# Turning the normed input by transposing DMAs instead of TensorE, in a fused convolution and gated-product kernel

## The chip, the cores and the metric

The kernel runs on one core of one Trainium2 chip. The core has TensorE (matrix products; the profile shows its matmuls as PE and its weight loads as PEld), VectorE (DVE), ScalarE (ACT), GpSimd (POOL) and SyncE (SP, which here only issues DMAs), and 16 DMA engines that all queues share. The metric is device time in microseconds of the whole launch. A time is given as the median of several executions; a profile is of one execution.

## The reference

The output is the sum of the input, a long convolution branch and a gated branch, both fed with the layer-normed input. Cut to what matters:

```python
x  = A_q                                   # 1 x 2048 x 640, bfloat16
xn = (x - mean(x)) / sqrt(var(x) + 1e-5)   # over the last axis

# A: short shift convolution of k (4 taps), times v, long convolution over 2048 tokens, times xn
kv = shift(k, shift_k) * v
y  = irfft(rfft(kv, 4096) * rfft(ssm_k, 4096))[:2048] + kv * ssm_D
A  = xn * y

# B: gated product
h  = sigmoid(xn @ w_gate) * (xn @ w_up)    # 640 x 1728 each
B  = h @ w_down                            # 1728 x 640

out = x + A + B
```

## The kernel before

**Layout.** Token 16 p + b lies on partition p in block b, so x and xn are tiles of 128 partitions x 16 blocks x 640 columns. Four blocks make a group (512 tokens), and there are four groups, t or g from 0 to 3. The 640 columns are five pieces of 128, counted by c, both as the contraction of the gated branch and as the five channel chunks of the convolution.

**Gated branch, by group.** `ln_norms`, `ln_var`, `ln_pow` and `ln_xn` norm a group's four blocks (VectorE, with one power on GpSimd). A product over columns needs the tokens of a block turned, columns on partitions. `xn_mm(g, i)` turns block i of group g by five TensorE transposes into a PSUM tile `pt`, and `xn_ev` copies it to `xnT[:, i]` on ScalarE. There is only one `xnT`, of four blocks; a group's turns write it after the last product of the group ahead has read it. Then 13 pairs `gate_mm`, `up_mm` (each five matmuls over 512 tokens) and one joint `both_mm` for the last 64 columns of both; `gate_ev` takes the sigmoid on ScalarE, `up_ev` multiplies on VectorE into `hT`. After that comes the group's down stage: eight `down_mm` products of 14 matmuls, in two pieces of seven each, evicted by `down_ev` (VectorE, added to x). The first group is handled ahead of the loop, with its turns between quarter products.

**Convolution branch, by chunk c.** It is a transform in two stages of matmuls. `kv_op` (16 VectorE steps) makes the shifted k times v, and `h_turn` rearranges the filter. `st1_mm` (8 steps of 8 matmuls) is the first stage; `st1_ev` evicts each to a tile `t`, `wr1` writes it to DRAM and `rd2` reads it back regrouped. `st2_mm` and `st2_ev` are the second stage, `prod` multiplies the spectra (VectorE), `inv1_mm`, `inv1_ev`, `wr2`, `rdb` and `inv2_mm` go back, and `inv2_q` and `inv2_x` multiply by xn and add to x. All evictions `st1_ev`, `st2_ev` and `inv1_ev` are ScalarE copies of 128x1024 f32.

**Order.** Each engine runs its instructions in program order. `step(k, fn, ...)` appends steps to chains by letter, and the string `ORDER` merges the chains by hand: each letter takes the next step of its chain. The letters F, J, I and Y take a step of B, C, A and E, but with its copy on VectorE; before's string has none of them. The SP queue issues nearly all DMAs, also in program order: a DMA that waits holds all that stand behind it.

**Letters that matter here.** g: gate, up, both and down products; s and u: their evictions; l and P: norms; e and E: `xn_mm` and `xn_ev` of groups 1 to 3; a and A, b and B, c and C: the three transform stages and their evictions; w, r, W, R: their DMAs; m, n, h, K, V, T: loads; k: `kv_op`; p: `prod`; d and q: `inv2`; o: stores.

**Buffers.** PSUM has two pools: `psC`, two buffers, for the transform stages (and the turns of the first group), and `psG`, four buffers, for products, down products, `inv2` and the turns of groups 1 to 3. The tiles `t1` and `t2` of the transform have two buffers each; `hn`, `sraw` and `dr` have one.

Of the kernel before, what the change touches and what calls it, by code (L numbers as in the profile page):

```python
# [10 lines left out]
BF16 = mybir.dt.bfloat16  # L11
# [8 lines left out]
P = 128  # L20
NB = S // P
NC = DM // P
# [35 lines left out]
def kernel(  # L58
# [14 lines left out]
    nc = tc.nc  # L73
# [17 lines left out]
    psC = ctx.enter_context(tc.tile_pool(name="psC", bufs=2, space=bass.MemoryType.PSUM))  # L91
    psG = ctx.enter_context(tc.tile_pool(name="psG", bufs=4, space=bass.MemoryType.PSUM))

    ident = res.tile([P, P], BF16, name="ident")
# [11 lines left out]
    xn = res.tile([P, NB, DM], BF16, name="xn")  # L106
    xnT = res.tile([P, 4, NC, P], BF16, name="xnT")
# [13 lines left out]
    sync = nc.sync  # L121
# [105 lines left out]

    xts = {}

    def xn_mm(g, i):  # L230
        pool, tag = (psG, "g") if g else (psC, "c")
        xts[i] = pt = pool.tile([P, NC, P], BF16, name="pt", tag=tag)
        for c in range(NC):
            nc.tensor.transpose(pt[:, c, :], xn[:, 4 * g + i, c * P:(c + 1) * P], ident[:])  # L234

    def xn_ev(g, i, copy=act_copy):
        copy(out=xnT[:, i, :, :], in_=xts[i][:, :, :])


    sig = {}  # L240
# [246 lines left out]
            nc.tensor.matmul(idle[:, :], lhsT=hT[:, 0, 0:P], rhs=hT[:, 0, :], start=True, stop=True)  # L487

    def turn(i):
        xn_mm(0, i)  # L490
        xn_ev(0, i)


    busy(15)
    for i in range(4):
# [5 lines left out]
        ln_pow(0, i, i + 1)  # L501
    ln_xn(0, 3)
    turn(0)
    busy(2)
    for i in range(4):
        for fc in range(2):
            for u in range(2):
                quarter(u, fc, i)
            if (i, fc) in ((0, 0), (1, 0), (1, 1)):
                turn(1 + i + fc)  # L510
# [2 lines left out]
        up_ev(0, fc)  # L513


    chains = {k: [] for k in "ABCDEHKPRTVWZabcdeghklmnopqrstuw"}

    def step(k, fn, *args):
        chains[k].append((fn, args))
# [88 lines left out]
    for g in range(1, 4):  # L608
        for i in range(4):
            step("l", ln_norms, g, i)  # L610
        step("l", ln_var, g, 0, 4)
        step("P", ln_pow, g, 0, 4)
        for i in range(4):
            step("l", ln_xn, g, i)
        for i in range(4):
            step("e", xn_mm, g, i)
            step("E", xn_ev, g, i)

    for b in range(0, 12, 2):
        step("o", store, b, b + 2, 0, 4 * P)  # L620
# [5 lines left out]
    step("o", store, NB - 1, NB, 4 * P, DM)  # L626

    ORDER = """
    mmmmmmmmmmZgmgsmgumgsmgugsgugsmgugskgkugkskgumkgsmkgumkgsmTguHgsHDgumgskkgukgskmgukgskgumkgkmgmutmkm
    auTaAHgAHDagAwlhauaAlglaglguwlgkPkgAulgAllleKeuKwEekaEekaEgkEVVHAgAHDgwughkgkugkskguKrrkaskaAgkAkguw  # L630
    gkskgutkgTskgkKuKaksaAKkgAkaugAwkaksaAkgkwakAgVuAVHasgwHDAauhgAkgkskwbugBrkgBkktbgpBrTkgBpsapsaAuguA
    apKgKswAkaugAkaKkwsakgVHAVgAuDHgswkcugCkgkskCgnuWakaAkgAkgukwbguBrlgBlgulbgBrlgBuglkPpgnulgllleenuEe
    kbEeprgEEgptkBgupBgkaauAgpAkapgswAkaugAkawksaAgkAkguwlcsglCgClbusgrlBWgBkugslpPkaauAgllAlglspwbgBruR
    kgBkscpguCpgCksWbkgBrugBkksbpgBrudBpdgsRqpcqgCqugCqpsWbgBrukgBspbgBrupdBadqsaApRgqAqapgwAqauseeEueaE
    egEEgAgAwaudAdqgwqRqcugCqgCguWbgBrgBugpbpdBrdqgBuqgqpcqgCupgCguWbgBrgBugpspRbgBrugBspcguCpgsCguWbsdr
    BdqgRBqqguqbpsgrBpgBugpspcgCugCsWbguBrdBgqspbqgBupgBspgucpsdCgRqRCqguWbsgBgBugpspgudsdqcqgCqoqdCudqg
    WqqgsqgugoguRRguggugguogodudqogqqogqdoudqogqqogqguogooouo
    """
    left = {k: iter(v) for k, v in chains.items()}
    for k in "".join(ORDER.split()):  # L640
# [33 lines left out]
```

## Time and profile before

| | us |
|---|---|
| median of 3 runs | 240.34 (239.64 to 241.22) |
| the profiled execution, whole | 240.16 |
| its span in the trace | 238.4 |
| TensorE, matmuls busy | 232.6 |
| VectorE busy | 190.5 |
| ScalarE busy | 140.9 |

The span runs from the first to the last instruction that the profiler records; the time of the whole execution has 1.8 us around it. The first product starts at about 8.3 us, when the first loads are in, and TensorE's last at 235.1. The granted TensorE clock is 1.00 throughout.

Matmuls of one kind that follow one another overlap: a transpose of 128x128 is recorded with 219 ns, and five of them in a row take 0.28 us in the chain. A product of five matmuls over 512 tokens takes 1.08 us. So a busy share of 98% does not mean that TensorE works at its peak, but an idle time in front of an instruction does mean that it waited.

The DMA issues are listed with their size and the median time from issue to landing; the queue's share of 16 engines' span counts the time of its packets.

### The profile page before, as it was taken

What the parts mean: (1) busy time and instruction counts of PE and PEld (TensorE: products, weight loads), DVE (VectorE), ACT (ScalarE), POOL (GpSimd) and SP (SyncE); (2) the same over time, 40 slices, a digit from 0 to 9 for tenths busy, and PEclk for the clock granted to TensorE, in tenths of its full rate; (3) what the DMA queues carried; (4) which work ended last, traced back from release to release, by engine and by line L of the source; (5) the groups of instructions that cost most, each with busy time, mean ns of one, the idle gap of its engine ahead of it and who ended that gap; (6) DMA issues with size and microseconds to landing.
All of it is one profiled execution on the core that took longest, in us unless ns stands there. A gap on an engine that the chain in (4) does not pass through costs nothing.

```text
span 238.4 us, 5555 instructions
## 1 busy us (share of the span) xinstructions
PE 232.6 (98%) x2265; PEld 134.8 (57%) x2265; DVE 190.5 (80%) x350; ACT 140.9 (59%) x178; POOL 11.2 (5%) x24
## 2 busy tenths in 40 slices
PE   8899999999999999999999999999999999999994
PEld 2664445877555555667754434577664434456772
DVE  4633989999999999999999999865585695968372
ACT  2343322728557898764888787997558858764000
POOL 5210000020000000002000000000000000000000
PEclk9999999999999999999999999999999999999999
DMA  7999999998998999998444889875849795285494
GB/s 213 291 315 236 254 326 294 197 257 236 251 312 252 259 292 292 297 252 313 154 179 143 235 237 265 216 231 202 230 119 223 186 282 126 83 241 145 123 303 137
DMA packets 89119, 54.82 MB, mean 230 GB/s; under 512 B 47814, under 2 KB 83206, under 8 KB 88838
## 3 DMA queue, kind: packets, MB, share of 16 engines
q1 hardware_dynamic: 88150, 53.66, 81.3%
q10 hardware_dynamic: 944, 0.82, 1.1%
q8 instruction: 17, 0.28, 0.5%
q14 instruction: 8, 0.07, 0.1%
HBM read 36.12 MB, written 18.35 MB: 228 GB/s over the span
## 4 chain that ended last, share of the span: by engine, by line
PE 91%; DMA 5%; ACT 2%; issue 0%; ACTq 0%; DVE 0%
PE pd L301 26%; PE pg L257 22%; PE pu L257 22%; PE psb L461 4%; PE ps L360 3%; PE ps L362 3%; PE ps L393 3%; DMA w<-in_B_w_up_dram 3%; PE psa L422 2%; PE pg L278 2%; PE pt L234 2%; DMA d<-t 2%; ACT t L223 1%; PE pu L248 1%; PE pg L248 1%
## 5 line engine op out<-in xcount | busy, mean ns | idle before, releaser
L257 PEld LDWEIGHTS <-w 128*128 128x128 bf16 x500 | 46.4, 98 | 54.4 <-issue 5.3
L301 PE MATMUL pd<-wd,hT 128*128 128x320 bf16 (+2 forms) x448 | 64.3, 299 | 0.0
L257 PE MATMUL pg<-xnT,w 128*128 128x512 bf16 x250 | 62.2, 379 | 0.0
L257 PE MATMUL pu<-xnT,w 128*128 128x512 bf16 x250 | 62.2, 379 | 0.0
L301 PEld LDWEIGHTS <-hT 128*128 128x128 bf16 x448 | 42.3, 98 | 18.5 <-issue 1.7
L266 ACT ACTIVATE sig<-pg 128x512 bf16<-128x512 f32 x52 | 31.3, 605 | 29.8 <-PE pg L257 28.0
L272 DVE TENSOR_TENSOR hT<-sig,pu 128x512 bf16<-128x512 bf16 x52 | 35.2, 680 | 15.5 <-PE pu L257 9.6
L223 ACT CAST t<-ps 128x1024 bf16<-128x1024 f32 x40 | 39.2, 1023 | 12.1 <-DMA d<-t 7.9
L223 ACT CAST xz<-ps 128x1024 bf16<-128x1024 f32 x40 | 38.5, 1017 | 10.6 <-PE ps L393 10.5
L306 DVE TENSOR_TENSOR x<-pd,x 128x320 bf16<-128x320 f32 (+2 forms) x32 | 15.3, 479 | 15.5 <-PE pd L301 15.3
L408 DVE TENSOR_TENSOR xz<-xz 128x2048 bf16<-128x2048 bf16 x20 | 24.3, 1217 | 0.2
L360 PE MATMUL ps<-kvh,S1t 128*128 128x128 bf16 x160 | 21.2, 217 | 0.5 <-ACT t L223 0.5
L362 PE MATMUL ps<-kvh,S1t 128*128 128x128 bf16 x160 | 21.2, 220 | 0.0
L340 DVE TENSOR_TENSOR acc<-acc,tmp 128x1024 bf16<-128x1024 bf16 x30 | 20.7, 689 | 0.6
L338 DVE TENSOR_TENSOR tmp<-kx,sc 128x1024 bf16<-128x1024 bf16 x30 | 20.5, 685 | 0.4
L223 ACT CAST ao<-psa 128x1024 bf16<-128x1024 f32 x16 | 15.6, 1014 | 6.0 <-PE psa L422 3.9
L362 PEld LDWEIGHTS <-S1t 128*128 128x128 bf16 x160 | 15.4, 96 | 2.9 <-issue 0.8
L466 DVE TENSOR_TENSOR yx<-psb,xn 128x512 bf16<-128x512 f32 x20 | 13.8, 690 | 3.9 <-PE psb L461 2.9
L360 PEld LDWEIGHTS <-S1t 128*128 128x128 bf16 x160 | 15.5, 97 | 2.3
L223 ACT COPY xnT<-pt 128x640 bf16<-128x640 bf16 x16 | 10.2, 708 | 10.9 <-PE pt L234 10.6
L198 DVE BATCH_NORM_STATS2 st<-x 128x6 f32<-128x320 bf16 x32 | 13.7, 470 | 2.6 <-DMA x<-in_A_q_dram 2.6
L406 DVE STREAM_SHUFFLE xz<-xz 128x512 f32<-128x512 f32 x20 | 14.5, 725 | 0.0
(44 smaller groups left out, 147.5 us busy)
## 6 DMA issues: line engine op xcount, KB each, us to landing
d<-t SPq DMA_DIRECT2D x20, 512.0 KB, 3.9
t<-d SPq DMA_DIRECT2D x20, 512.0 KB, 5.2
bi<-d SPq DMA_DIRECT2D x8, 512.0 KB, 5.2
d<-ao SPq DMA_DIRECT2D x6, 512.0 KB, 4.1
kx<-in_A_k_dram SPq DMA_DIRECT2D x10, 256.0 KB, 5.1
hn<-in_A_ssm_k_dram SPq DMA_DIRECT2D x20, 128.0 KB, 5.9
kvh<-in_A_v_dram SPq DMA_DIRECT2D x10, 256.0 KB, 5.3
x<-in_A_q_dram SPq DMA_DIRECT2D x3, 640.0 KB
```

The source lines that it names most:

```text
L223: nc.scalar.copy(out=out, in_=in_)
L257: nc.tensor.matmul(pg[:, :], lhsT=w[:, c, u * UP + fc * P:u * UP + (fc + 1) * P], rhs=xnT[:, :, c, :], start=(c == 0), stop=(c == NC - 1))
L266: nc.scalar.activation(sig[fc][:, :], pgs[0, fc][:, :], ACT.Sigmoid)
L272: nc.vector.tensor_tensor(hT[:, fc, :], sig[fc][:, :], pgs[1, fc][:, :], ALU.mult)
L301: nc.tensor.matmul(pd[:, :], lhsT=hT[:, fc, bb * P:(bb + 1) * P], rhs=wd[:, fc, es], start=(fc == 0), stop=(fc == NFC - 1))
L306: nc.vector.tensor_tensor(x[:, 4 * t + bb, es], pds[bb, half][:, :], x[:, 4 * t + bb, es], ALU.add)
L338: nc.vector.tensor_tensor(d["tmp"][:, :, :], kx[:, lo + 3 - m:hi + 3 - m, :], sb(m), ALU.mult)
L340: nc.vector.tensor_tensor(d["acc"][:, :, :], d["acc"][:, :, :], d["tmp"][:, :, :], ALU.add)
L360: nc.tensor.matmul(ps[:, i, 0:P], lhsT=S1[:, b, h, :], rhs=cin[c]["kvh"][:, 0, b, :], start=True, stop=True)
L362: nc.tensor.matmul(ps[:, i, P:2 * P], lhsT=S1[:, b, h, :], rhs=hp[:, b // 2, b % 2, :], start=True, stop=True)
L406: nc.vector.stream_shuffle(z[:, 2, :, :].bitcast(F32), z[:, 1, :, :].bitcast(F32), swap)
L408: nc.vector.tensor_tensor(z[:, 1:3, :, :], z[:, 0:1, :, :].to_broadcast((P, 2, 8, P)), z[:, 1:3, :, :], ALU.mult)
```

## The change

The turns of groups 1 to 3 are made by a transposing DMA on the SP queue, one for each block of 128 tokens x 640 columns, from `xn` straight to `xnT`. The 12 `xn_mm` and 12 `xn_ev` steps go, with their PSUM tiles; the turns of group 0 remain as they were. Letter E is gone, and e now stands for the DMA.

The order string is another one, in all its length. Each chain keeps its own order; what differs is how the chains are merged. Fourteen evictions now run on VectorE: seven `inv1_ev` (J), five `st2_ev` (F) and two `st1_ev` (I).

```diff
-    def xn_mm(g, i):
-        pool, tag = (psG, "g") if g else (psC, "c")
-        xts[i] = pt = pool.tile([P, NC, P], BF16, name="pt", tag=tag)
+    def xn_mm(i):
+        xts[i] = pt = psC.tile([P, NC, P], BF16, name="pt", tag="c")
         for c in range(NC):
-            nc.tensor.transpose(pt[:, c, :], xn[:, 4 * g + i, c * P:(c + 1) * P], ident[:])
+            nc.tensor.transpose(pt[:, c, :], xn[:, i, c * P:(c + 1) * P], ident[:])
-    def xn_ev(g, i, copy=act_copy):
-        copy(out=xnT[:, i, :, :], in_=xts[i][:, :, :])
+    def xn_ev(i):
+        nc.scalar.copy(out=xnT[:, i, :, :], in_=xts[i][:, :, :])
+    def xn_turn(g, i):
+        sync.dma_start_transpose(xnT[:, i, :, :], xn[:, 4 * g + i, :])
...
         for i in range(4):
-            step("e", xn_mm, g, i)
-            step("E", xn_ev, g, i)
+            step("e", xn_turn, g, i)
```

Where the turns stand, in the order of the SP queue around them (st1, st2 and gate steps are TensorE's, at their place in the string):

| group | before | after |
|---|---|---|
| 1 | `xn_mm` 0 to 3 after the down pieces of block 2, between `st1_mm(0, 5)` and `st1_mm(0, 7)` | SP: wr1(0,1), load h of chunk 2, **turns 0 to 3**, wr1(0,2); turn 3 stands between `st1_mm(1, 1)` and the first gate product |
| 2 | after the down pieces of block 2, around `st2_mm(4)` | SP: load k of chunk 4, wr1(2,2), **turn 0**, rd2(3), wr1(2,3), load h of chunk 4, rd2(4), **turns 1 to 3**, wr1(3,0), rd2(5) |
| 3 | ahead of the down products, around `st1_mm(4, 6)` | SP: rd2(11), **turn 0**, wr1(4,1), rdb(1,0), rd2(12), **turns 1 to 3**, rdb(1,1) |

Other steps that change their place among the chains: in group 1's down stage `st1_mm(0, 0)` to `st1_mm(0, 3)` stand between the first down pieces, not behind four of them; `st1_mm(1, 0)` and `st1_mm(1, 1)` go ahead of the first gate product of group 1; `ln_norms` of group 1 go ahead of the first four `down_ev`, and its four `ln_xn` stand among `kv_op` and `down_ev` steps, not in a row; the norms of group 2 go ahead from the down stage of group 1 into its products. The first `rd2` moves from gate product 1 to gate product 5 of group 1; `st2_mm(0)` stays behind up product 7. `prod` 9 and 10 and three `inv2` evictions move from group 2's products to its down stage. The loads of h, k, v and taps of chunks 2 to 4 mostly come later in the SP queue, among the `wr1` and `rd2` steps, and those of x of groups 2 and 3 earlier. The first 19 loads keep their order.

More of the change, by code (lines that the diff above doesn't have):

```diff
@@ L489, in turn @@
     def turn(i):
-        xn_mm(0, i)
-        xn_ev(0, i)
+        xn_mm(i)
+        xn_ev(i)
     busy(15)
@@ L513 @@
         up_ev(0, fc)
-    chains = {k: [] for k in "ABCDEHKPRTVWZabcdeghklmnopqrstuw"}
+    chains = {k: [] for k in "ABCDHKPRTVWZabcdeghklmnopqrstuw"}
     def step(k, fn, *args):
@@ L628 @@
     ORDER = """
[L629 to L637, printed above, removed]
+    mgmmmmgmgmgsummZmgmgsmmgugmssgkmmukgskgugkusgsugkkgkHggmmuskuggkHmssukgmDgggukskgukkksaTmmgauAgmkaAH
+    HlglAalAlglmwgautAkagugmggPmwlkgAhglkelauleggkakukkugekAAuuDkHgkuaaekgkwgsATKugkAwgsnkkgskgtuKaKAuka
+    gskkgauwgkAlDAakVgglkKkrsakAuwAgakgVsAgalswAkaguKgkkAurbgkBswksHgTBgkbtuguBBpkgawkgslaAgsuKkalupKgrA
+    AgkahPlnHsAwugaglVasgkgVpAsTAKukDpuckwglkkCgaCaHAugkAkgkeklubkgrkBBgguuwkgbggkpghtBBrbkegleBgBaauegw
+    HAparguVkApauAkgwpADWaugakksAngkugpkwlAsucgsgJlpkCulbrgBKBsgaAuapgpAgrbsFggBussWkukrlpcHgguPCCgbslkV
+    ggBuBgbpslBkuBRdpgspgWqqcusdgCgkrkkrCsbqFugqBgubskgBRdwBuagpAaqAdgllWwrsewRpugaqgIaggrpAaAaqupgIqupg
+    ddcCgeuqgJebgupegFRuBgqbBpgqBgWpdcrguqqgJqCrubwuwdrgFpBgsbqpggpWpqBugBpscsuJggCurpgbggRFBbsWpdsudupq
+    rgBqgqBcqRJsgrpCgsbBuWguBpdspqgbuBBgpqdpsgcgrugCRJqbpggsduBqsBgupgspgWqRqcuJdqgsgCdoqgusqWgudggqgugo
+    uRgquRggddouqqgguqddgqqqqoquqggoogouoogouoooo
     """
```

## The prediction

> **What bounds the kernel now.** I read the page's busy times, the chain of waits that ended last, and then the busy times by stage, cut where one group's products end and its down products begin.
>
> ```profile
> PE 232.6 (98%) x2265; PEld 134.8 (57%) x2265; DVE 190.5 (80%) x350; ACT 140.9 (59%) x178; POOL 11.2 (5%) x24
> ...
> q1 hardware_dynamic: 88150, 53.66, 81.3%
> ...
> PE 91%; DMA 5%; ACT 2%; issue 0%; ACTq 0%; DVE 0%
> ```
>
> TensorE is 91% of the chain, and the 5% of DMA is mostly the load before the first product (1.65 to 8.89 us). In the waits TensorE's own idle times add up to under 3 us. By stage (window, its length, then busy us of PE, PEld, DVE, ACT, POOL with counts, granted clock, DMA share, GB/s):
>
> ```profile
> 39.40:59.40 20.00, 20.00 (x198) 15.69 (x196) 19.63 (x40) 11.29 (x14) 2.17 (x3) 1.00 0.90 236
> 59.40:98.00 38.60, 38.11 (x329) 20.66 (x327) 37.40 (x58) 28.28 (x36) 0.84 (x2) 1.00 1.01 275
> 98.00:117.00 19.00, 19.00 (x205) 13.59 (x204) 18.64 (x42) 12.24 (x15) 1.39 (x1) 1.00 0.88 284
> 117.00:158.00 41.00, 41.00 (x455) 20.83 (x452) 39.56 (x76) 35.12 (x43) 1.01 (x1) 1.00 0.72 205
> 158.00:180.00 22.00, 22.00 (x294) 15.16 (x292) 12.13 (x24) 14.37 (x18) 0.00 (x0) 1.00 0.64 188
> 180.00:217.00 37.00, 37.00 (x418) 17.04 (x417) 28.07 (x48) 27.07 (x34) 0.00 (x0) 1.00 0.68 184
> ```
>
> Two things are to be seen. TensorE has no gap to close in any stage, so only work taken off it can win. And from 39.4 to 158 VectorE works 115.2 of 118.6 us and the DMA engines are near full until 117: both are nearly as tight as TensorE.
>
> **What leaves TensorE.** Transposes in the chain, in order of time (start, us, what):
>
> ```profile
> 53.58 0.84 PE pt L234 x15
> 54.87 0.28 PE pt L234 x5
> 55.60 3.80 PE pd L301 x28
> 59.41 1.08 PE pg L257 x5
> ...
> 111.33 0.84 PE pt L234 x15
> ```
>
> A block's five transposes hold TensorE for 0.28 us. Twelve blocks go: 12 x 0.28 = **3.36 us** off the path that sets the end, 1.12 at each group change. ScalarE also loses 12 copies, 8.5 us, hidden, since it is busy 59%. The shapes and durations that price the rest:
>
> ```profile
> L223 ACT CAST t<-ps 128x1024 bf16<-128x1024 f32 x40 | 39.2, 1023 | 12.1 <-DMA d<-t 7.9 <-PE ps L362 3.3 <-ACT xz L223 0.7
> L466 DVE TENSOR_TENSOR yx<-psb,xn 128x512 bf16<-128x512 f32 x20 | 13.8, 690 | 3.9 <-PE psb L461 2.9
> L223 ACT COPY xnT<-pt 128x640 bf16<-128x640 bf16 x16 | 10.2, 708 | 10.9 <-PE pt L234 10.6
> ```
>
> ```profile
> t<-d SPq DMA_DIRECT2D x20, 512.0 KB, 5.2
> hn<-in_A_ssm_k_dram SPq DMA_DIRECT2D x20, 128.0 KB, 5.9
> x<-in_A_q_dram SPq DMA_DIRECT2D x1, 160.0 KB, 3.0
> ```
>
> **What a turning DMA costs.** No transposing DMA is in the trace. From below: 160 KB cut like the k and v loads into runs of 128 columns (256 bytes) is 640 runs. Queue q1 spent 0.813 x 16 x 238.4 us on 88150 packets, 35 ns each, so 640 runs over 16 engines take 1.41 us (an estimate). From issue to landing the nearest rows are 3.0 us (same 160 KB, short queue) and 5.9 us (hn, full queue). I take 1.41 us of transfer each, one after another, and about 3 us to landing, since the size is that of x; the range keeps 5.9.
>
> The Trainium skill ("VectorE: DVE Perf Modes", "The three transpose paths") lists 1309 ns for a 128x128 block turned by DMA against 390 on TensorE; five one after another would be an estimated 6.5 us for each of the twelve turns. Its page "Advanced Engine Details and Errata" ("X-Bar Transpose (TRN2)") says instead that such DMAs are as fast as ordinary ones, 350 to 400 GB/s, an estimated 0.5 us. No row of before decides between them, and the sum uses neither.
>
> **Where the turns stand, and who waits.** All four of a group must land before its first gate product, which reads all 512 tokens.
> *Group 1.* In before the last ln_xn ends at 54.0 us. In after the norms come ahead of four down_ev (0.48 each, 1.9 us earlier), but ln_xn is spread among kv steps, so it is again about 54, and the first about 51. The first gate product moves from 59.24 by -1.12 (transposes) and +0.9 (two st1 steps now ahead of it, 0.45 each) to about 59.0. That leaves the last turn 5.0 us. Landing in 3 us costs nothing; 5.9 costs 0.9; in series at 3.0 from 51 costs 4. I take 0.5. Behind the turns in SP's queue stands wr1(0,2), which in before was issued at 54.8, so it is hardly later.
> *Group 2.* Turns 1 to 3 stand in SP's queue behind rd2(4), which must wait for st2(2) to free its buffer. From there TensorE has ten down pieces of seven matmuls (0.95 each in the chain), two st2 (0.36, and 0.11 more on the product behind) and three st1 (eight matmuls 0.056 apart, 0.45): 11.8 us to the first gate product. SP needs some 1.8 us to issue rd2(4) (two such took 3.66 at 103.3), it lands 5.2 later, and three transfers of 1.41 follow: 11.2. Just in time, with nothing for the turns' own landing; between 0 and 3 late, I take 0.8. wr1(3,0) and rd2(5) wait behind them in the queue, with st2(5), behind gate product 3, as their first reader.
> *Group 3.* Three turns follow rd2(12), about 11.5 us of TensorE work ahead of the gate, and the DMA share is 0.64: 0.
>
> **What the new order moves.** Fourteen evictions of 128x1024 f32 go from ScalarE to VectorE: three while group 2's products run, six in its down stage, five in group 3's products. Each costs between 1.02 us (ScalarE's CAST of this shape) and 1.38 (twice the 690 ns of 512 columns from PSUM); I take 1.2, as the latter row is the same engine and part of it is fixed. In the down stage of group 2 VectorE then has 12.13 + 6 x 1.2 + 5.4 (prod 9 and 10, 1.94 each, and three inv2 evictions, 1.53, that came earlier before) = 24.7 us, against TensorE's 22.0 - 1.12 + 3 x 0.45 = 22.2. That is 2.5 over (1.4 to 3.6 by the two prices). Four psG buffers (one per product or down pair of pieces) let VectorE trail by about 1.9 us (two pieces), and group 3's products have room (28.07 + 6.0 of 36), so TensorE sees 0 to 3; I take 0.8. Elsewhere VectorE hides behind TensorE, but in 39.4 to 158 only 118.6 - 2.24 - 115.2 = 1.2 us of cover stays.
> Loads of chunks 2 to 4, x of groups 2 and 3 and wr1 move in SP's queue. The first rd2 passes from gate 1 to gate 5 of group 1 while its st2 stays behind up 7; five products (5.4) and four st1 (1.8) lie between, the t2 tile lands in 5.2, so 0, else one wait of 1 to 2. The early loads keep their order on SP. The tail after the last product (235.1 to 238.4) is unchanged: 0.
>
> **Sum.** -3.36 + 0.5 + 0.8 + 0.8 = -1.3 us on the profiled execution's 240.16 (span 238.4 plus 1.8 around it) = 238.9. That execution lies 0.2 under the median of 240.34, so the forecast is **239.1**. About 1% (2.4 us) is what a measurement can tell from no change.
>
> **Rivals.**
> *All hidden*: turns land in 3 us, VectorE's excess sits in the buffers; 240.34 - 3.36 = 237.0. For it: the group 1 and 3 margins. Against it: three resources tight at once, and no stage with room until 158.
> *Slow turns*, the case on the other side: the turns run one after another and hold SP's queue. At 4 us each group 1 ends at 51 + 16 = 67 against 59.0 (+8.0), group 2 has 1.8 for rd2(4) and three turns, 13.8 against 11.8 (+2.0), group 3 12 against 11.5 (+0.5): 237.0 + 10.5 = 247.5. At the 5.9 us of hn's row it is +15.6, +7.7 and +6.2: 266.5. It decides from about 3.4 us a turn: +5.6, +0.2 and 0, less the 3.36 saved, make the 2.4 of the 1% band. For it: near-full DMA engines at the first two group changes and landings of 5 to 6 us. Against it: a run of short transfers overlaps its latencies (four hn loads issue within 1.8 us). The 1309 ns of the skill's page for each 128x128 block leads to this case.
> *Queue order*: each turn costs only its 1.41 us, but SP's other steps wait behind turns that wait for ln_xn; wr1 and rd2 come 3 to 4 us later at two group changes and TensorE waits that long for st1 or st2: 237.0 + 7 = 244. For it: ScalarE already waited 7.9 us for wr1.
> *VectorE as the bound*: +3.6 in group 2's down stage and the 1.2 of cover used up: 237.0 + 4 = 241, no measurable change.
> That the turns are not made by DMA is excluded by the edit; 20 transposes must remain.
>
> **Chances.** All hidden 0.32. Forecast 0.24 and VectorE as the bound 0.08, together 0.32 within 1%. Slow turns 0.26 and queue order 0.10, together 0.36 slower. The likeliest case with a narrow time of its own is the forecast's band around 239.1 (237.9 to 242). The range runs from 236.6, a little under all hidden, to 246, which takes in the queue case and turns of about 3.8 us; beyond lie the slower turns, under 2 in 10.
>
> **What would show it.** L234 x20 and xnT copies x4. For the forecast: gaps of TensorE under 1.5 us just before the first gate product of groups 1 and 2, released by a DMA of xnT from xn, and some wait for VectorE at 160 to 180. All hidden: none of these, and TensorE's end 3.4 us earlier. Slow turns: gaps of several us there, SPq busy for us on the turning line, landings over 4 us. Queue order: the gaps at st1 or st2, released by t or d. The forecast is wrong if the turns' landing is far from 3 us in either direction, or if the evictions cost VectorE's order more than its buffers hide.

## The result, and the profile after

| | before | after |
|---|---|---|
| median of 18 runs each, one chip | 239.82 (239.37 to 241.22) | 238.94 (237.94 to 240.44) |
| ratio, with its 95% interval | | 0.9956 (0.9939 to 0.9973) |
| the profiled execution | 240.16 | 237.94 |
| its span | 238.4 | 236.2 |

So the gain is 0.9 us by the medians and 1.1 by the ratio, with an interval from 0.65 to 1.46 us (239.82 x 0.0027 and x 0.0061). It is real and lies within the 1%. Ratios leave out executions over 1.5% above the fastest of their kernel, which are only two in this document: 240.83 us (the profiled one) and 394.24 us of the kernel before with its turns left out. The profiled execution of after is the lowest of its 18, 1.0 under their median, and that of before is 0.3 above its median, so the two traces differ by 2.2 us where the medians differ by 0.9.

Busy times, the large DMA queue (packets, MB, share of 16 engines) and the chain that ended last, from the page of after:

```profile
PE 229.1 (97%) x2205; PEld 131.2 (56%) x2205; DVE 204.1 (86%) x364; ACT 121.7 (52%) x152; POOL 11.5 (5%) x24
...
q1 hardware_dynamic: 96214, 55.62, 90.3%
...
PE 84%; DVE 8%; DMA 4%; issue 1%; ACT 0%; ACTq 0%; DVEq 0%
```

TensorE lost 60 transposes and 3.5 us of busy time, and 7% of the chain. VectorE gained 13.6 us, and now 8% of the chain is its own. All DMA queues together have 8064 packets more, 672 for each of the 12 turns. Queue q1's engines worked 0.903 x 16 x 236.2 = 3413 us against 0.813 x 16 x 238.4 = 3101 before: 311 us more, or 1.6 us of all 16 engines for each turn, if the other DMAs took what they took before. In the experiment that issues the turns from ScalarE's queue q10, that queue's share goes from 1.1% to 7.3% by the turns alone, and the same sum gives 1.3 us.

The turns themselves, in the view of the tile `xnT` of after (ns min/median/max on the issuing queue, then from issue to landing):

```profile
L240 SPq DMA_TRANSPOSE xnT<-xn x12: 1215/1254/2492, 53.4 to 164.4; - x12
...
DMA to landing us min/median/max: 2.6/4.4/6.2
```

A turn holds SP's queue for 1.25 us. The trace has the landing of five of the twelve: 3.3 and 2.6 us after the issue in group 1, 4.4 to 6.2 in groups 2 and 3. What TensorE waited for in the places that the change touches (us in all, times, longest):

```profile
PE pg L260 <- DMA xnT<-xn: 0.9, 1, 0.9
PE pu L260 <- DVE hT L275: 0.8, 1, 0.8
```

and the stages, cut at the same events as before (columns as in the prediction):

```profile
59.00:96.00 37.00, 35.30 (x270) 18.73 (x267) 34.27 (x63) 25.10 (x33) 2.15 (x3) 1.00 0.98 275
96.00:116.00 20.00, 20.00 (x235) 13.31 (x233) 19.70 (x35) 13.42 (x16) 1.16 (x1) 1.00 1.05 238
116.00:156.00 40.00, 40.00 (x427) 19.60 (x425) 38.65 (x70) 29.96 (x38) 1.01 (x1) 1.00 0.95 252
156.00:179.00 23.00, 23.00 (x302) 15.91 (x300) 22.09 (x37) 9.59 (x10) 0.00 (x0) 1.00 1.01 256
```

TensorE has one stage with gaps, group 1's products: 37.00 - 35.30 = 1.70 us, which is the two waits, 0.93 and 0.77. Groups 2 and 3 have none. The trace adds up: -3.36 (transposes) + 0.93 + 0.77 = -1.66, and TensorE's last product ends at 233.3 instead of 235.1; the tail behind it is 0.4 shorter, which makes the span's 2.2. Two smaller changes cancel: TensorE waits 0.5 us longer for the first weights, and a wait of 0.5 us for ScalarE, which before had in group 1's products, is gone.

**Where the 0.93 comes from.** SP's queue in after (start, length on the queue, line, what):

```profile
50.55 0.26 SPq L136 DMA_DIRECT2D dr<-in_A_ssm_D_dram  x1
50.90 2.35 SPq L139 DMA_DIRECT2D hn<-in_A_ssm_k_dram  x4
53.36 5.27 SPq L240 DMA_TRANSPOSE xnT<-xn  x4
...
62.16 2.63 SPq L155 DMA_DIRECT2D kx<-in_A_k_dram  x2
```

VectorE wrote the normed blocks from 50.40 to 53.52, so the first turn could have gone at about 50.8. It went at 53.36, since load h of chunk 2 stands ahead of it, and that load needs the single buffer `dr`, which `add_D(1)` on GpSimd reads last. GpSimd's own order in after:

```profile
49.11 1.02 POOL L214 TENSOR_TENSOR rstd<-var,mhalf 128x4 f32<-128x4 f32 x1 [17.25 <-DVE var L210]
50.10 0.42 POOL L317 TENSOR_TENSOR kvh<-kvh,dr 1x128 bf16<-1x128 bf16 x1
```

`add_D(1)` (L317) stands behind group 1's power (L214), which waits for the variances. In before it ran ahead of the power, and the same loads left 3.8 us earlier:

```profile
45.28 0.43 POOL L314 TENSOR_TENSOR kvh<-kvh,dr 1x128 bf16<-1x128 bf16 x1 [11.07 <-DVE kvh L320]
46.71 0.26 SPq L136 DMA_DIRECT2D dr<-in_A_ssm_D_dram  x1
```

Now they leave at 50.55, the fourth turn is issued at about 57.4 and lands at 60.0, and the gate product starts at 60.05, 0.93 after TensorE is free.

**Where the 0.77 comes from.** The k load of chunk 2 is further back in the same queue and leaves at 62.16. On VectorE:

```profile
69.21 0.69 DVE L337 TENSOR_TENSOR acc<-kx,sc 128x1024 bf16<-128x1024 bf16 x1 [1.73 <-DMA kx<-in_A_k_dram]
```

VectorE stands idle for 1.73 us in a stage where it is busy 93% of the time, falls behind with the `up_ev` steps that free the psG buffers, and up product 6 of group 1 (counted from 0; the expectations below call it 5) waits for it until 77.73. Both waits are argued from the trace so far; the first experiment tests them together.

### The profile page after: what moved, and what is told of

It reads as the page before. It is cut to its first block, busy times and chain, and to the rows that moved or that the text cites. A ratio compares the mean times of both kernels' runs of the same rounds, so it can differ in the third digit from the quotient of the medians.

```text
span 236.2 us, 5433 instructions
## 1 busy us (share of the span) xinstructions
PE 229.1 (97%) x2205; PEld 131.2 (56%) x2205; DVE 204.1 (86%) x364; ACT 121.7 (52%) x152; POOL 11.5 (5%) x24
## 4 chain that ended last, share of the span: by engine, by line
PE 84%; DVE 8%; DMA 4%; issue 1%; ACT 0%; ACTq 0%; DVEq 0%
PE pg L260 23%; PE pu L260 23%; PE pd L304 20%; PE psb L464 4%; PE ps L396 3%; DMA w<-in_B_w_up_dram 3%; PE ps L363 3%; PE ps L365 3%; PE psa L425 2%; PE pg L281 1%; DVE st L198 1%; DVE tmp L341 1%; DMA xnT<-xn 1%; DVE acc L343 1%; PE pu L251 1%
## 5 line engine op out<-in xcount | busy, mean ns | idle before, releaser
L304 PE MATMUL pd<-wd,hT 128*128 128x320 bf16 (+2 forms) x448 | 65.3, 299 | 0.0
L223 ACT CAST t<-ps 128x1024 bf16<-128x1024 f32 x38 | 37.8, 1016 | 23.6 <-PE ps L365 16.0
L223 ACT CAST xz<-ps 128x1024 bf16<-128x1024 f32 x35 | 34.2, 1015 | 20.3 <-PE ps L396 20.3
L365 PE MATMUL ps<-kvh,S1t 128*128 128x128 bf16 x160 | 21.7, 220 | 0.0
L363 PE MATMUL ps<-kvh,S1t 128*128 128x128 bf16 x160 | 21.6, 218 | 0.0
L223 ACT CAST ao<-psa 128x1024 bf16<-128x1024 f32 x11 | 10.8, 1014 | 5.8 <-PE psa L425 5.6
L464 PEld LDWEIGHTS <-TBt 128*128 128x128 bf16 x160 | 9.8, 98 | 3.0 <-issue 1.5
```

Of the source, the lines that this page charges most:

```text
L223: nc.scalar.copy(out=out, in_=in_)
L304: nc.tensor.matmul(pd[:, :], lhsT=hT[:, fc, bb * P:(bb + 1) * P], rhs=wd[:, fc, es], start=(fc == 0), stop=(fc == NFC - 1))
L363: nc.tensor.matmul(ps[:, i, 0:P], lhsT=S1[:, b, h, :], rhs=cin[c]["kvh"][:, 0, b, :], start=True, stop=True)
L365: nc.tensor.matmul(ps[:, i, P:2 * P], lhsT=S1[:, b, h, :], rhs=hp[:, b // 2, b % 2, :], start=True, stop=True)
L464: nc.tensor.matmul(ps[:, i, :], lhsT=TB[:, h, 4 * m + i, :], rhs=bi[:, h, 4 * (m % 2) + i, :], start=(h == 0), stop=(h == 1))
```

## The experiments

Theory: the turns are nearly free where SP issues them early enough; what is lost in after is lost in group 1, through `add_D(1)` and what queues behind it. Rivals: the DMA engines' work for the turns, VectorE with its 14 more evictions, and SP's queue being held by the turns. All ratios are to the kernel before on the same chip, with 95% intervals.

### One letter: add_D(1) ahead of the power

Group 1's power (P) stays; D moves from behind it to behind the `h_turn` that it follows.

```diff
-    HlglAalAlglmwgautAk...AAuuDkHgkuaaekgkwgs...
+    HDlglAalAlglmwgautAk...AAuukHgkuaaekgkwgs...
```

> Changed kernel with one step of POOL's queue moved: add_D(1) ahead of ln_pow(1). In the changed kernel add_D(1) ran at 50.1 us behind ln_pow(1), so h of chunk 2 was issued at 50.6 to 53.3 and the four turns behind it began at 53.4, 2.5 us after their first block was normed. Theory (the turns start late in SP's queue, and the loads behind them too): the turns begin at about 50.9, the last lands by 57.4, TensorE's 0.93 us before the first gate product of group 1 is gone, the k load of chunk 2 goes out some 2 us earlier and the 0.77 us at up product 5 shrinks or goes; 0.9 to 1.7 us less than the changed kernel, ratio to before 0.989 to 0.992. Rival (the transfers of the four turns set the time, not their start): the wait stays at 0.5 us or more, ratio 0.994 to 0.997.

Measured: 237.03 us, ratio 0.9881 (0.9864 to 0.9899). SP's queue in this kernel:

```profile
47.29 0.26 SPq L136 DMA_DIRECT2D dr<-in_A_ssm_D_dram  x1
47.64 2.15 SPq L139 DMA_DIRECT2D hn<-in_A_ssm_k_dram  x4
51.09 6.01 SPq L240 DMA_TRANSPOSE xnT<-xn  x4
```

The loads leave 3.3 us earlier, the turns 2.3 us, and the four of them now wait for nothing but the norms. Both of TensorE's waits are gone, that at up product 6 too, with the k load 1.5 us earlier (60.61). In the stretch of both TensorE now idles 0.32 us in all (columns as above):

```profile
59.00:98.00 39.00, 38.68 (x299) 21.02 (x296) 37.77 (x68) 27.79 (x36) 2.16 (x3) 1.00 0.95 267
```

The interval lies wholly below that of after, and the ratio just below the range that was expected. One letter triples the gain, 2.9 us (2.4 to 3.3), and the time beats both kernels. As the one edit removes both waits, their shares are the trace's.

### The same turns on another queue

```diff
-        sync.dma_start_transpose(xnT[:, i, :, :], xn[:, 4 * g + i, :])
+        nc.scalar.dma_start_transpose(xnT[:, i, :, :], xn[:, 4 * g + i, :])
```

> Changed kernel with the twelve turning DMAs issued from ScalarE's queue, at the same places in the order, instead of SP's. Theory (SP's queue, held 1.25 us by each turn and by the load ahead of them, is what costs): group 1's turns begin when a block is normed (50.8), no wait at its first gate product, k of chunk 2 is issued about 5 us earlier, no wait at up product 5; 1.7 us less than the changed kernel, ratio 0.989. Rival: each turn holds ScalarE for the same 1.25 us and its evictions behind come late, so TensorE waits at st1 or st2 for a free psC buffer by 1 to 4 us: ratio 0.998 to 1.01.

Measured: 249.04 us, ratio 1.0388 (1.0371 to 1.0405), the opposite of what freeing SP's queue should give. ScalarE and its queue around group 1's turns:

```profile
51.07 3.99 ACTq L240 DMA_TRANSPOSE xnT<-xn  x3
55.17 1.01 ACT L223 CAST t<-ps 128x1024 bf16<-128x1024 f32 x1 [5.64 <-DVE acc L343]
56.54 1.01 ACT L223 CAST t<-ps 128x1024 bf16<-128x1024 f32 x1 [0.35 <-PE ps L365]
56.54 1.47 ACTq L240 DMA_TRANSPOSE xnT<-xn  x1
```

Three turns leave 2.3 us earlier than in after. The fourth stands behind two evictions in ScalarE's own order, which put it off by 1.5 us (from 55.06, where the third is through, to 56.54); it still leaves 0.87 us earlier than in after. But it lands far later. The turn in the chain of after, and then of this kernel (start, us to landing):

```profile
57.41 2.60 DMA xnT<-xn
56.54 7.58 DMA xnT<-xn
```

With 2.60 us it would have landed at 59.14, before TensorE is free at 59.31. So the 4.95 us for which TensorE idles come from the late landing, not from the order of issue. Why it took so long stays open: from 61 to 62 us, with the turn still unfinished, hardly a transfer began (DMA share 0.02). Behind the idle time TensorE works at half clock to about 68.7. In group 3 three turns hold ScalarE until 180.01, and TensorE waits for the eviction behind them, which is the rival's mechanism:

```profile
174.09 5.92 ACTq L240 DMA_TRANSPOSE xnT<-xn  x3
180.38 1.01 ACT L223 CAST xz<-ps 128x1024 bf16<-128x1024 f32 x1 [5.29 <-issue]
181.45 0.66 PE L396 MATMUL ps<-t,SMt 32*32 32x512 bf16 x16 [2.13 <-ACT xz L223]
```

Whether SP's held queue is the cost can't be judged from this. What it shows is that a turn that leaves earlier need not land earlier, and that a turn also holds up the engine that issues it.

### The new order with TensorE's turns

The body of `xn_turn` does all four turns of a group at the place of the second:

```diff
-        sync.dma_start_transpose(xnT[:, i, :, :], xn[:, 4 * g + i, :])
+        if i != 1:
+            return
+        for j in range(4):
+            pt = psG.tile([P, NC, P], BF16, name="pt", tag="g")
+            for c in range(NC):
+                nc.tensor.transpose(pt[:, c, :], xn[:, 4 * g + j, c * P:(c + 1) * P], ident[:])
+            nc.scalar.copy(out=xnT[:, j, :, :], in_=pt[:, :, :])
```

> The new order and its fourteen VectorE evictions kept, the DMA turns undone: the four turns of a group on TensorE with ScalarE copies, all at the place of the group's second turn. Theory (the transposes are worth 3.36 us and the DMA gives 0.9 to 1.7 of it back): 1.7 to 2.5 us slower than the changed kernel, ratio to before 1.002 to 1.007. Rival (the gain comes from the new merging of the chains, the turns are even): the changed kernel's 0.996 or less.

Measured: 244.61 us, ratio 1.0223 (1.0201 to 1.0246), well above what was expected. TensorE's waits:

```profile
PE pt L245 <- DVE x L315: 3.2, 3, 1.9
```

The turns take psG buffers between down pieces, and the down evictions on VectorE free them late. As a test of the order alone it says too much, since four turns in a row at one place bring a wait of their own; the next one spreads them.

### TensorE's turns at the DMA turns' own places

As above, without the first two added lines and the loop: each turn stands where its DMA stood.

> The changed kernel with each DMA turn replaced at its own place by five transposes on TensorE and a ScalarE copy. In pe_turns_new_order (four turns of a group at one place) TensorE waited 4 us for psG buffers that down_ev had not freed and for the copies, besides 3.36 us of transposes. Theory (the new order has no room for TensorE turns in its places, since a turn takes a psG buffer, and its last turn of group 1 stands next to the first gate product): 3.36 plus 1 to 3 us slower than addD_ahead's floor, 241 to 244 us, ratio 1.005 to 1.018. Rival (only the bunching cost): 3.36 over 237.0, ratio 1.000 to 1.004.

Measured: 246.00 us, ratio 1.0248 (1.0208 to 1.0289). Again above the expectation, now with TensorE's waits spread over five lines of 0.7 to 1.8 us each; they add up to 5.2 us, most of the 6.3 by which the span is longer than before's (244.7 against 238.4). So the new order doesn't carry the gain: with TensorE's turns in it, it is some 6 us slower than before. These two don't part the order's own cost from that of the places given to the turns.

### The old order with DMA turns

```diff
-            step("e", xn_mm, g, i)
-            step("E", xn_ev, g, i)
+            step("e", xn_turn, g, i)
+            step("E", int)
```

> The kernel before with the DMA turns alone, in its own order, at the places of its TensorE turns; all evictions on ScalarE. Theory (the order was needed to give the turns time): in group 1 turns 1 to 3 stand behind wr1(0,2) (54.8 us), go out to 58 and land at 60.5, against a first gate product at 58.1: 2.4 us of wait; in group 2 they go out from 111.3 at 1.25 us each and land at 119 to 121 against 116.5: 2.4 to 4.2; group 3 none; less 3.36: 1.4 to 4 us slower than before, ratio 1.006 to 1.016. Rival (the places don't matter): 0.99 to 0.997.

Measured: 249.36 us, ratio 1.0411 (1.0367 to 1.0454), beyond the expectation. SP's queue at group 1 in this kernel:

```profile
53.21 1.31 SPq L241 DMA_TRANSPOSE xnT<-xn  x1
54.57 0.56 SPq L159 DMA_DIRECT2D kx<-in_A_k_dram  x1
55.19 0.47 SPq L160 DMA_DIRECT2D kx<-in_A_k_dram  x1
55.76 1.21 SPq L241 DMA_TRANSPOSE xnT<-xn  x1
...
58.31 2.92 SPq L241 DMA_TRANSPOSE xnT<-xn  x2
```

The last turn is issued at about 60.0, and TensorE wants the tile at 58.5: 4.70 us of waiting at group 1 and 3.95 at group 2, and none at group 3.

```profile
PE pg L260 <- DMA xnT<-xn: 8.7, 2, 4.7
```

The expectation had the waits at 4.8 to 6.6 us and no more. Behind each of the two gaps the granted clock is 0.50, to about 68.3 and 129.7 by the means of its 2 us slices; the five matmuls of the gate product take 2.29 us. The sum closes: -3.36 + 8.7 leaves 4.4 of the 9.7 us by which the span grew (238.4 to 248.1), and TensorE at half speed from 63.2 to 68.3 and from 126.3 to 129.7 loses 0.5 x (5.1 + 3.4) = 4.3.

### DMA turns in the old order, group 3 alone

```diff
-            step("e", xn_mm, g, i)
-            step("E", xn_ev, g, i)
+            step("e", xn_turn if g == 3 else xn_mm, g, i)
+            step("E", *((int,) if g == 3 else (xn_ev, g, i)))
```

> The kernel before, its order and its ScalarE evictions kept, with DMA turns in group 3 alone; groups 1 and 2 stay on TensorE. There the turns stand 11 to 13 us of TensorE work ahead of the first gate product, and in dma_turns_old_order that gate showed no wait. Theory (time between issue and need decides): 20 transposes go for nothing, 1.1 us less than before, ratio 0.993 to 0.998. Rival (a DMA turn in the old order costs wherever it stands, by the rdb, wr1 and wr2 steps it holds in SP's queue): 1.002 to 1.01.

Measured: 238.75 us, ratio 0.9953 (0.9938 to 0.9968). SP's queue:

```profile
156.97 5.33 SPq L241 DMA_TRANSPOSE xnT<-xn  x4
```

The four leave by 162.3, the first gate product is at 178.26, and nothing waits for them. A third of the transposes, 4 x 0.28 = 1.12 us, brings 1.1 us (239.83 x 0.0047). That is as much as the whole change brought, without a new order or an eviction moved. In the same old order group 3's turns are all gain and those of groups 1 and 2 bring 8.7 us of waits, so it is the time between issue and need that decides, not the DMA as such.

### The turns left out

In the order with D ahead, `xn_turn` returns at once:

> addD_ahead with the twelve turning DMAs left out (groups 1 to 3 are multiplied with group 0's turned tokens; the output isn't the reference's). Theory (once they start in time the DMA turns are hidden whole): the same as addD_ahead within 0.4 us, ratio to before 0.986 to 0.990. Rival (their 1.25 us each on SP's queue and 1.6 us each on the 16 DMA engines still cost): 0.5 to 2 us less, ratio 0.980 to 0.986.

Measured: 236.40 us, ratio 0.9849 (0.9814 to 0.9883), against 0.9881 with the turns; spans of the profiled executions 234.9 without and 234.7 with them. So twelve turns, 1.3 to 1.6 us of 16 engines each, 15 to 19 us in all, cost some 0.8 us together by the ratios, which differ by 0.0032; the intervals overlap, and taken together they leave room for none or for 1.7 us (an estimate from the two). The ratio lies in the range given to the rival and not in the theory's, so the times don't refute it. The traces speak against it: with the turns TensorE's only wait behind the first products is 0.2 us, though the DMA share is near 1.00 from 59 to 179 us, and the two spans differ by 0.2. But one of the two executions is on the low side of its kernel's and the other on the high side. Nearly all of the DMA engines' work for the turns is hidden; whether all of it is, stays open.

In the kernel before, with both of the turns' steps replaced by nothing:

> The kernel before with the turns of groups 1 to 3 left out (TensorE transposes and ScalarE copies; the output isn't the reference's), in its own order. Theory (twelve times five transposes at 0.28 us are the whole price of the TensorE turns): 3.36 us less than before, ratio 0.984 to 0.988. Rival 1 (VectorE, 97% busy from 39 to 158 us, takes over as the bound): 1 to 2.4 us less, ratio 0.990 to 0.996. Rival 2 (the turns also cost by the psG buffers they hold): 4 us less or more, ratio 0.983 or below.

Measured: 237.79 us, ratio 0.9891 (0.9851 to 0.9930), 1.7 to 3.6 us less. The 3.36 us of the prediction lie inside, near the end; the ratio itself lies between the theory's range and that of the first rival, and the interval is too wide to part a gain of 3.36 from a clearly smaller one. Its profiled execution, of 240.83 us, is 3.0 us above the median and can't stand for the time; it comes up again below, for its clock.

### The evictions back on ScalarE

In the order with D ahead, all copies of F, J, I and Y go to ScalarE:

```diff
-        fn(*args, **({"copy": dve_copy} if k in "FJIY" else {}))
+        fn(*args, **({"copy": act_copy} if k in "FJIY" else {}))
```

> addD_ahead with the fourteen VectorE evictions given back to ScalarE at the same places: VectorE loses 17 us, ScalarE gains 14. Theory (VectorE's added load is hidden, and so is ScalarE's): within 0.7 us of addD_ahead, ratio 0.985 to 0.991. Rival 1 (VectorE is the hidden bound of group 2's down stage): 1 us less or more, ratio 0.984 or below. Rival 2 (two evictions of one step in a row on ScalarE hold the sigmoids and the psC buffers behind them): 1 to 4 us more, ratio 0.993 to 1.005.

Measured: 237.98 us, ratio 0.9926 (0.9896 to 0.9957); VectorE's busy time falls to 189.5 us and ScalarE's rises to 134.0. It is about 1 us slower than with the evictions on VectorE (0.9881), with intervals that touch and on another chip; the ratio is just beyond the theory's range and short of the second rival's. So VectorE's added work isn't what holds the kernel, and that rival falls; if anything the move to VectorE helps. TensorE's waits here are 0.8 for VectorE and 0.4 for ScalarE in the convolution's stages.

### One and two turns more

In the kernel after, block 0, or blocks 0 and 1, of group 1 are turned once more behind the fourth turn:

```diff
         sync.dma_start_transpose(xnT[:, i, :, :], xn[:, 4 * g + i, :])
+        if (g, i) == (1, 3):
+            for j in range(1):
+                sync.dma_start_transpose(xnT[:, j, :, :], xn[:, 4 + j, :])
```

> The changed kernel, with block 0 of group 1 turned a second time behind that group's fourth turn. Theory (a turn holds SP's queue 1.25 us, and group 1's gate waits for the last landing): the wait before the first gate product grows from 0.93 to about 2.2 us, the loads behind go out 1.25 us later, so 1.3 to 2.5 us slower than the changed kernel, ratio to before 1.000 to 1.007, with the granted clock at 1.00. If an idle time of 2 us lowers the clock already, as 4.0 and more did in dma_turns_old_order and act_queue: 3 us more, ratio 1.013 to 1.02. Rival (turns overlap in the DMA engines, the hold isn't what counts): wait under 1.3 us, ratio 0.995 to 0.998.

> The changed kernel, with blocks 0 and 1 of group 1 turned a second time behind that group's fourth turn. Theory: the wait before the first gate product is about 3.4 us; with the clock kept 2.5 to 4.5 us slower than the changed kernel, ratio 1.006 to 1.015; with the clock halved for some 6 us behind the wait, as after the 4.0 and 4.7 us of dma_turns_old_order, 3 us on top, ratio 1.018 to 1.028. Rival (turns overlap): under 1.002.

Measured with one more: 240.44 us, ratio 1.0018 (0.9995 to 1.0042). TensorE's first gate product of group 1:

```profile
60.92 1.25 PE L263 MATMUL pg<-xnT,w 128*128 128x512 bf16 x5 [1.91 <-DMA xnT<-xn]
```

The wait grows from 0.93 to 1.91, that is by 0.98, for a turn that holds the queue for 1.24; the first turn also left 0.46 us earlier than in after (52.90). The time is 1.5 us above that of after (by ratios, 0.0062 x 239.8), for the loads behind are later too: up product 6 waits 0.97 instead of 0.77, and an st1 step 0.7. The queue's hold goes on to the end of the kernel once the slack is used up.

Measured with two more: 241.91 us, ratio 1.0095 (1.0068 to 1.0123). The same product, and the stretch around it (columns as above):

```profile
63.20 2.29 PE L263 MATMUL pg<-xnT,w 128*128 128x512 bf16 x5 [3.42 <-issue]
```

```profile
62.00:63.00 1.00, 0.00 (x0) 0.00 (x0) 0.89 (x2) 0.00 (x0) 0.00 (x0) 0.75 0.73 165
63.00:64.00 1.00, 0.80 (x2) 0.28 (x3) 0.00 (x0) 0.00 (x0) 0.00 (x0) 0.50 1.04 393
...
65.00:66.00 1.00, 1.00 (x4) 0.30 (x3) 0.00 (x0) 0.47 (x1) 0.00 (x0) 0.54 0.33 68
```

The profile doesn't name the landing that ended the wait. The idle time is 3.42 us, and the clock falls to 0.50 some 2.7 us into it (a mean of 0.75 in the slice from 62 puts the fall at 62.5; the idle time began at 59.8) and is back at 1.00 by 66. The median fell into the band that had been given for a kept clock, and yet the clock fell: of its 3.4 us at half speed 0.7 lay in the idle time, so it cost TensorE only 0.5 x 2.7 = 1.4 us, less than had been supposed.

The Trainium skill, "TensorE: Matmul & The Clock Gate", section "Why this matters for your kernels", advises against idle gaps of TensorE over some 3 us between bursts, as they bring the clock back to half. The runs agree only in part. Gaps of 3.42, 3.95, 4.70 and 4.95 us brought it to 0.50, and 1.91 us here and 1.92 us in the new order with TensorE's turns did not. But on ScalarE's queue 2.13 us did too:

```profile
182.00:184.00 2.00, 2.00 (x24) 1.14 (x9) 2.00 (x4) 1.81 (x2) 0.00 (x0) 0.50 1.21 279
```

And in the profiled execution of the kernel before without turns two waits of 1.1 and 0.5 us between 161 and 164 us were followed by 0.50 from 164.5 to 167.9. So the length of a single gap doesn't decide it in these traces. Each stretch at half clock lasts 3.4 us (from 62.5, 126.3, 164.5 and 181.4) or twice that (from 61.4 in the old order, from 61.9 on ScalarE's queue).

## Why the prediction was right, and where its steps were off

The forecast was 239.1 us, the sum -1.3 us; the medians give 238.94 and -0.9 (-0.65 to -1.46). The mechanism held in its outline: TensorE sets the time, the transposes come off it, and part of that goes back in waits. That the number was met to 0.2 us is luck: of the three waits in the sum only one came, larger than taken, and one more came where the sum had nothing. The parts of the sum, by its steps:

- **What leaves TensorE, -3.36.** Right in size: group 3 alone brought 1.1 where 1.12 was due, all turns left out 1.7 to 3.6.
- **What a turn costs the DMA engines, 1.41 us.** 1.3 to 1.6 measured. The estimate counted 640 runs; the trace shows 672 packets. A difference of this size is not seen in the time, as the experiment without turns shows.
- **About 3 us to landing.** Right in group 1, where the sum used it: 3.3, 2.6 and, for the fourth turn, 2.60. In groups 2 and 3, where nothing hung on it, 4.4 to 6.2. The hold of 1.25 us on SP's queue was no term of the sum, but the 1.41 us of transfer that the working put one after another stood in its place: four turns take 5.27 us, 1.3 each.
- **Group 1, 0.5.** 0.93. The landing was not the step that failed, as turn 4 took 2.60 us. "The first about 51" was: it left at 53.36. "The early loads keep their order on SP" was true, and missed that a load's place in SP's queue says nothing about when its buffer is free. The edit moved `add_D(1)` behind the power on GpSimd, which held back load h of chunk 2 ahead of the turns, and the prediction didn't follow GpSimd's queue at all. With one letter the first turn leaves at 51.09 and the wait is 0.
- **Group 2, 0.8.** 0. The working put the landing of rd2(4), 5.2 us, ahead of the turns, in series; SP doesn't wait for a landing before it issues the next DMA. rd2(4) held the queue for 0.38 us (105.64), the three turns left from 106.06 to 111.20, and the gate product is at 117.26.
- **Group 3, 0.** 0.
- **VectorE in group 2's down stage, 0.8.** No wait there. An eviction takes 1.22 us on VectorE where 1.2 was taken, and the durations of all 37 instructions in 156 to 179 add up to 25.0, near the 24.7 worked out. But the same 37 run from 155.8 to 179.4 us, and VectorE is busy for 22.7 of them: neighbouring instructions overlap in the records, here by 2.3 us in 37, 0.06 each. In the 23.0 us of the stage VectorE is busy 22.09. The step that failed is the adding of single durations as if each began at the end of the last.
- **What the new order moves, 0.** 0.77, at up product 6 of group 1, through the late k load of chunk 2. The sum's 0.8 for VectorE and this 0.77 are nearly equal by chance: same engine, other place, other cause.

So the errors cancelled in part: 0.5 + 0.8 + 0.8 = 2.1 was forecast as given back, 1.70 was seen, all of it in group 1.

Of the rivals, *all hidden* came true one letter further on: 237.03 measured, 237.0 worked out. *Slow turns* fell: 1.25 us a turn on the queue, against the 3.4 from which it decides. The Trainium skill's 1309 ns for a 128x128 block turned by DMA ("VectorE: DVE Perf Modes", "The three transpose paths") doesn't add up over a larger turn here: five such blocks in one DMA hold the queue for 1254 ns in the median and land 2.6 to 6.2 us after the issue, against the prediction's 6.5 by adding. *Queue order* is near the mechanism that acted, with the turns themselves behind a load that waits, but at 1.7 us, in one group, not 7 in two; in the old order it is 8.7 us of waits, and slower than that rival's time. *VectorE as the bound* fell.

What stays open: how much of the 6 us by which the new order with TensorE's turns is slower than before is the order's own and how much comes from the places of the turns; why the fourth turn took 7.58 us to land from ScalarE's queue; and whether the 0.8 us between the order with D ahead and the same without turns is anything but scatter.

## What to carry to other kernels

Price a DMA that takes an engine's place by the time from when its queue can issue it to when its result is needed, and follow each buffer that a DMA ahead of it in the queue waits for, back to its last reader, on every engine, also the one that is 5% busy. Where a DMA's slack is short, try the change only in the places where it is long: group 3 alone gave the whole gain without a new order. A gap of TensorE can cost more than its own length, through the clock behind it: every gap from 2.13 us up did here, those of 1.91 and 1.92 us did not.

## What the hardware showed that was not expected

- A turning DMA of 128x640 holds its queue 1.25 us (1.2 to 2.5), the plain DMAs just ahead of and behind group 1's turns 0.26 to 0.81 us each. A second turn meets the hold of the queue, not the landing of the first: four turns left within 5.27 us, though one takes 2.6 us and more to land.
- From ScalarE's queue the turn that ended TensorE's wait landed 7.58 us after its issue, from SP's in after 2.60. Of the other turns there the trace has only two landings (4.8 and 6.3 us), too few to say that this queue is slower in general.
- The clock fell to 0.50 some 2.7 us into an idle time of 3.42 us, and also after one of 2.13; it stayed there for 3.4 us, or for 6.8 where the idle time was 4.70 or 4.95.
- Neighbouring VectorE instructions overlap in the records, by 0.06 us each in a stretch of 37, so a full VectorE does more than the sum of its rows says.
